# State attention in front of two expert layers on one core: score products on 64x32 array tiles, the state softmax by a GpSimd subtraction and an exponential out of PSUM

## Chip, cores and metric

The kernel runs on one core of one Trainium2 chip. The metric is the device time of one execution in microseconds: the median of 3 runs of the kernel before is 488.5 us (487.32 to 489.64).

## What is computed

Three layers in float32. The first is an attention between tokens and 32 state vectors per head, in both directions; its output, 512 token rows and 32 state rows for each of 8 batches (4608 rows of 512), goes through a soft mixture of 8 experts and then through a gated linear unit.

```python
# x: (8, 8, 512, 64) batches, heads, tokens, width; state: (8, 8, 32, 64)
scores = scale * x @ state.T
a = softmax(scores, axis=-1)           # over the 32 states
xread = a @ state
a2 = softmax(scale * state @ x.T, -1)  # over the 512 tokens
sread = a2 @ x
x = concat([xread, sread], axis=2)     # then rows x (heads * width) = 4608 x 512
logits = x @ phi                       # 32 slots, 4 for each expert
slot_input = softmax(logits, 0).T @ x
slot_out[e] = relu(slot_input[e] @ w1[e]) @ w2[e]
x = softmax(logits, 1) @ slot_out
out = (silu(x @ w_gate) * (x @ w_val)) @ w_out
```

Both softmaxes subtract their maximum and divide by the sum plus 1e-9.

## The kernel before

The order of the work on every engine is the order of the program text: the whole kernel is written under a manual schedule, so that each engine (TensorE, ScalarE, VectorE, GpSimd and SyncE, which issues the loads) carries out its instructions in the order in which the lines call them, and waits by semaphores for what it needs.

**Attention.** The loop of line 979 takes batches b = 0 to 6; a step of it works on batch b and finishes pieces of b-1 and b-2. `scores` (line 232) multiplies stB, the state vectors of a pair of heads laid on the diagonal of a 128x64 block with zeros beside them, with the transposed tokens xT: four products of 512 columns, two on each half of the array's columns. ScalarE copies the scores with the scale into the tile sts (line 240). `load_T` (line 216) makes xT for batches 3 to 7 on chip, by 16 transposes of xn and two copies of 1024 columns, half 0 on VectorE, half 1 on ScalarE (line 230); for batches 0 to 2 it is loaded. From sts two softmaxes start:

- over the tokens (a2): `scores_max` (line 243) takes the negated maximum along the rows on VectorE, `state_exp` (line 248) gives the exponential with that bias and with the sum as accumulator, in two halves on ScalarE, `state_tr` (line 304) transposes the result on TensorE and copies it out, `sread_mm` multiplies it with xn and `sread_out` (line 330) with the reciprocal of the sums, which `sread_recip` (line 311) has made, into srC;
- over the states (a): `attn_sub` (line 263) transposes the scores, takes the maximum over each 32 and subtracts it (two VectorE passes of 1024 columns), `attn_exp` (line 273) gives the exponential on ScalarE, the sum and its reciprocal on VectorE and the normalisation on GpSimd (line 286), `attn_tr` (line 338) transposes a and copies it for the logits.

`logits_mm`, `logits_max`, `logits_exp`, `logits_tr`, `slots_mm` and `slots_out` make the slot softmax of the token rows of a batch, one or two steps later; `sr_T`, `sr_mm`, `sr_exp` and `sr_tr` do it for the state rows, four batches at a time. In batch 0 the product SP of stB and phi is made as well (line 1012). `build_stB` (line 394) fills stB for four batches, by two copies of 64 partitions each. The last batch (from line 1029) is written out by itself: there the softmax over the states goes in halves of 512 columns (`half_sub`, `half_exp`, `half_at`), and the normalisation of half 0 is GpSimd's, of half 1 VectorE's (line 1063).

**PSUM.** `pbig` hands out three buffers of two banks in turn, `psmall` two of one bank.

**Loads.** `push` makes the list of all loads in order: tokens, w1 and w2 of the two expert groups, the weights of the gated unit. `pump` issues what has room: 17 ring places of 8 KB a partition (`rg`), which come free with `done()`, and the tiles named in `spots`, which hold parts of w1 of (group, index) (0, 2) to (0, 7), (1, 0) and (1, 1) in working tiles as they come free; a tag in `late` is not used before `free(tag)` is called. The loads are issued by SyncE in that order.

**Experts.** From line 1198: `expert_1` multiplies the slot inputs with w1, `expert_2` with w2; the first preparations of the gated unit run beside them. **Main loop.** From line 1348: 17 blocks of 256 rows, 6 pairs of column blocks of the gated unit; the change does not touch it, except for the tag of a converted weight tile (line 646).

Of the kernel before, what the change touches and what calls it, by code (L numbers as in the profile page):

```python
# [50 lines left out]
XT_PE = (3, 4, 5, 6, 7)  # L51
ROWS = S + NS
# [13 lines left out]
def attn_moe_glu_kernel(  # L66
# [36 lines left out]
    stB = wk.tile([128, B, 4, 64], F32, tag="A", name="stB")  # L103
# [34 lines left out]
    late = {"x", "A", "a2", "sts", "e2", "a0", "at"}  # L138
# [34 lines left out]
    def push_pair(q):  # L173
# [40 lines left out]
    xT = {}  # L214

    def load_T(b, half):
        if b >= B or b not in XT_PE:
            return
        x_ = got["xn", b]
        if half == 0:  # L220
            xT[b] = rg.tile([128, 4, S], F32, tag="u", name="xT")
            room[0] -= 1
            if b == XT_PE[-1]:
                room[1] = 0
        p = pbig([128, 2, S])
        for kk in range(2):
            kc = 2 * half + kk
            for j in range(4):
                pe.transpose(p[:, kk, j * 128:(j + 1) * 128], x_[:, j, kc * 128:(kc + 1) * 128], ident)
        (act.copy if half else dve.tensor_copy)(out=xT[b][:, 2 * half:2 * half + 2, :], in_=p)  # L230

    def scores(b):
        x_ = xT.pop(b) if b in XT_PE else got.pop(("xt", b))
        p = pbig([128, 2, S])
        for pr in range(4):
            r = 64 * (pr % 2)
            pe.matmul(out=p[r:r + 64, pr // 2, :], lhsT=stB[:, b, pr, :], rhs=x_[:, pr, :], start=True, stop=True)  # L237
        done()
        t = wk.tile([128, 2, S], F32, tag="sts", bufs=1, name="sts")
# [23 lines left out]
    def attn_sub(b):  # L263
        t = sts[b]
        v = tr8([t[:, 0, :], t[:, 1, :]]).rearrange("p j (h s) -> p (j h) s", s=NS)
        m1 = sm.tile([128, 32], F32, tag="m1", name="m1")
        dve.tensor_reduce(out=m1, in_=v, axis=AX.X, op=ALU.max)  # L267
        a = wk.tile([128, 4, 256], F32, tag=f"a{b % 3}", name="a")
        av = a.rearrange("p j (h s) -> p (j h) s", s=NS)
        dve.tensor_tensor(out=av, in0=v, in1=bc(m1, NS), op=ALU.subtract)  # L270
        A[b] = a

    def attn_exp(b, part=True):
        a = A[b]
        av = a.rearrange("p j (h s) -> p (j h) s", s=NS)
        if part is not None:
            act.activation(out=a, in_=a, func=AF.Exp)  # L277
        if part is False:
            return
        z = sm.tile([128, 32], F32, tag="z", bufs=1, name="z")  # L280
        dve.tensor_reduce(out=z, in_=av, axis=AX.X, op=ALU.add)  # L281
# [3 lines left out]
        if part:  # L285
            pool.tensor_tensor(out=av, in0=av, in1=bc(r, NS), op=ALU.mult)  # L286
        else:
            RZ["a"] = r

    def attn_norm(b):  # L290
        av = A[b].rearrange("p j (h s) -> p (j h) s", s=NS)
        dve.tensor_tensor(out=av, in0=av, in1=bc(RZ.pop("a"), NS), op=ALU.mult)
# [11 lines left out]
    def state_tr(b, eng=act):  # L304
        e = E2T.pop(b)
        p = tr8([e[:, 0, :], e[:, 1, :]])
        t = e.rearrange("p q s -> p (q s)").rearrange("p (j n) -> p j n", j=4)
        (act.copy if eng is act else dve.tensor_copy)(out=t, in_=p)
        E2N[b] = t

    def sread_recip(b):
        z = RZ.pop(b)
        dve.tensor_scalar(out=z, in0=z, scalar1=EPS, scalar2=None, op0=ALU.add)
        r2 = sm.tile([128, 2], F32, tag="r2", name="r2")
        dve.reciprocal(out=r2, in_=z)
        RZ[b] = r2

    def sread_mm(b):
        x_, e = got.pop(("xn", b)), E2N.pop(b)
        p = psmall([128, 2, D])  # L320
        for q in range(2):
            for j in range(4):
                for c in range(4):
                    h = 4 * q + c
                    pe.matmul(out=p[32 * c:32 * c + 32, q, :], lhsT=e[:, j, h * 32:h * 32 + 32], rhs=x_[:, j, h * 64:h * 64 + 64],
# [4 lines left out]
    def sread_out(b):  # L330
        p, r2 = P4.pop(b), RZ.pop(b)
        o = 32 * (b % 4)
        for c in range(4):
            dst = srC[o:o + 32, b // 4, :, :].rearrange("p (q c) d -> p q c d", c=4)[:, :, c, :]
            cc = slice(32 * c, 32 * c + 32)
            dve.tensor_tensor(out=dst, in0=p[cc], in1=bc(r2, D)[cc], op=ALU.mult)  # L336
# [57 lines left out]
    def build_stB(g):  # L394
# [3 lines left out]
        v = p.rearrange("p r (b s) -> p b r s", s=NS)  # L398
        for hh in range(2):
            r = slice(64 * hh, 64 * hh + 64)  # L400
            dve.tensor_copy(out=stB[r, 4 * g:4 * g + 4, :, NS * hh:NS * hh + NS], in_=v[r])
# [240 lines left out]
    def split_wo(q, t, sc):  # L642
        if q == 2:
            w = bqm[:, 0:1024].bitcast(F16).rearrange("p (a n) -> p a n", a=2)
        else:
            w = wk.tile([128, 2, 1024], F16, tag=("at", "a2", "", "sts", "C", "stn")[q], bufs=1, name="wo16")
# [305 lines left out]
    with tc.manual_schedule():  # L952
# [10 lines left out]
        dve.memset(stB, 0.0)  # L963
# [15 lines left out]
        for b in range(B - 1):  # L979
# [4 lines left out]
            if ok(b - 1):  # L984
                sread_recip(b - 1)
# [6 lines left out]
            at(b, 1)  # L992
            state_exp(b)
            if ok(b - 1):
# [3 lines left out]
            at(b, 2)  # L998
            attn_sub(b)
            at(b, 3)  # L1000
            if ok(b - 1):
                attn_tr(b - 1)
            at(b, 4)
            state_tr(b)
            at(b, 5)
            attn_exp(b)
            if b == 0:
                p = psmall([128, B, 2, NSL])
                for bb in range(B):
                    for pr in range(4):  # L1010
                        r = 64 * (pr % 2)
# [399 lines left out]
```

## Time and profile before

| | |
|---|---|
| median of 3 runs | 488.5 us |
| the profiled execution | 489.95 us, of which 488.2 us are its span |
| TensorE busy | 461.4 us (95%) |
| VectorE busy | 322.8 us (66%) |
| ScalarE busy | 260.2 us (53%) |
| GpSimd busy | 156.8 us (32%) |
| chain that ended last | TensorE 71%, VectorE 19%, ScalarE 5% of the span |

Busy time is the time in which an engine works on an instruction; matmuls are pipelined, so TensorE's is not the time at its peak. The chain that ended last is followed back from the last instruction of the program to what released each step; an engine's share of it says how much of the span hung on that engine.

### The profile page before, as it was taken

To read this page: it belongs to the slowest core of one execution; us is meant where nothing else is said; L and a number is where in the kernel's file an instruction comes from. 1 tells how busy PE (TensorE), PEld (TensorE's weight loads), DVE (VectorE), ACT (ScalarE), POOL (GpSimd) and SP (SyncE) were. 2 spreads that over 40 slices of the span, in tenths; PEclk is the share of its full clock that TensorE was granted. 3 is DMA by queue.
4 is the path that set the end of the run, shared out by engine and by line. 5 is a ranking of instruction groups with operands and counts; after the bars stand their busy time and mean duration, and the time that the engine had idled before them with its cause. 6 is when DMAs were issued, how large, how long until landed. Compare 5 with 4: busy or idle time off the path is not lost.

```text
span 488.2 us, 9003 instructions
## 1 busy us (share of the span) xinstructions
PE 461.4 (95%) x3543; PEld 253.2 (52%) x3543; DVE 322.8 (66%) x614; ACT 260.2 (53%) x452; POOL 156.8 (32%) x134
## 2 busy tenths in 40 slices
PE   7889999899898999998999899899999999999996
PEld 6666667645355454454455354455555555555553
DVE  3888888657618866768989878876433344344454
ACT  1677676634405988777456365545444444444441
POOL 0111221128013434343343243342433333333331
PEclk9999999999899999999999999999999999999999
DMA  8999985969999820202000000000011112112124
GB/s 300 425 416 411 419 338 207 348 234 367 421 401 418 367 87 2 64 23 79 9 1 1 0 1 0 2 1 1 0 44 43 45 43 68 63 45 76 54 86 173
DMA packets 16363, 74.23 MB, mean 152 GB/s; under 512 B 1601, under 2 KB 3009, under 8 KB 9665
## 3 DMA queue, kind: packets, MB, share of 16 engines
q1 hardware_dynamic: 16320, 73.65, 38.6%
q8 instruction: 28, 0.46, 0.4%
q14 instruction: 15, 0.11, 0.1%
HBM read 64.73 MB, written 8.91 MB: 151 GB/s over the span
## 4 chain that ended last, share of the span: by engine, by line
PE 71%; DVE 19%; ACT 5%; issue 2%; DMA 1%; POOL 0%; SPq 0%; DVEq 0%; ACTq 0%; POOLq 0%
PE p L1296 48%; PE p L1262 8%; PE p L483 3%; PE p L514 3%; DVE nm L245 2%; DMA u<-in_xt_dram 1%; DVE srC L336 1%; DVE sh L1267 1%; DVE gvf L569 1%; DVE a L270 1%; DVE z L281 1%; PE s L734 1%; DVE xT L230 1%; DVE m L267 1%; PE p L237 1%
## 5 line engine op out<-in xcount | busy, mean ns | idle before, releaser
L1296 PE MATMUL p<-wo,hl 128*128 128x512 f16 x1020 | 235.1, 379 | 4.4 <-DVE osb L1307 3.3
L1276 POOL TENSOR_TENSOR hl<-sh,hl 128x512 f16<-128x512 f32 x102 | 125.4, 1229 | 202.4 <-ACT hl L1275 112.8
L1296 PEld LDWEIGHTS <-hl 128*128 128x128 f16 x1224 | 119.1, 98 | 129.9 <-issue 4.6
L1267 DVE SCALAR_TENSOR_TENSOR sh<-p,segk,sh 128x512 f32<-128x512 f32 x102 | 76.4, 749 | 93.8 <-ACT sh L1263 85.3
L1275 ACT CAST hl<-sh 128x512 f16<-128x512 f32 x102 | 62.9, 617 | 115.3 <-PE p L1296 80.9
L1263 ACT ACTIVATE sh<-p,sg 128x512 f32<-128x512 f32 x85 | 58.3, 686 | 5.7 <-PE p L1262 1.0
L1307 DVE SCALAR_TENSOR_TENSOR osb<-p,segm,osb 128x512 f32<-128x512 f32 x62 | 45.3, 747 | 10.9 <-PE p L1296 10.9
L1296 PE MATMUL p<-bqm,hl 128*128 128x512 f16 x204 | 46.8, 379 | 0.0
L1262 PE MATMUL p<-cstack,gvs 128*128 128x256 f16 x272 | 41.2, 273 | 2.4 <-DVE gvs L892 1.3
L1262 PEld LDWEIGHTS <-gvs 128*128 128x128 f16 x272 | 25.9, 98 | 20.5 <-issue 3.2
L286 POOL TENSOR_TENSOR a<-a,r 128x1024 f32<-128x1024 f32 x7 | 13.4, 1914 | 68.1 <-DVE md L363 48.9
L1262 PE MATMUL p<-cstack,gv 128*128 128x256 f16 x136 | 20.6, 273 | 0.9 <-DVE segm L807 0.9
L1305 ACT ACTIVATE osb<-p,segk 128x512 f32<-128x512 f32 x26 | 17.2, 693 | 3.3 <-PE p L1296 3.0
L569 DVE SCALAR_TENSOR_TENSOR gvf<-u,gvf 128x512 uint32<-128x512 uint32 (+1 forms) x22 | 18.6, 860 | 0.1
L1262 PEld LDWEIGHTS <-gv 128*128 128x128 f16 x136 | 13.0, 98 | 10.1 <-issue 1.7
L573 DVE SCALAR_TENSOR_TENSOR gvf<-u,gvf 128x512 uint32<-128x512 uint32 (+1 forms) x22 | 18.1, 843 | 0.1
L514 PE MATMUL p<-u,exq 128*32 128x256 f32 x256 | 15.4, 382 | 0.7 <-ACT exq L504 0.7
L253 ACT ACTIVATE e<-sts,nm 128x512 f32<-128x512 f32 x16 | 11.4, 715 | 8.2 <-DVE nm L245 8.2
L563 ACT ACTIVATE gvf<-u 128x512 f32<-128x512 f32 (+1 forms) x22 | 15.3, 716 | 0.0
L240 ACT ACTIVATE sts<-p 128x1024 f32<-128x1024 f32 x7 | 7.2, 1025 | 12.8 <-PE p L237 12.8
L281 DVE TENSOR_REDUCE z<-a 128x32 f32<-128x1024 f32 x7 | 8.5, 1220 | 8.1 <-ACT a L277 8.1
L566 DVE TENSOR_SCALAR gvf<-gvf 128x512 uint32<-128x512 uint32 (+1 forms) x22 | 12.1, 565 | 1.5 <-ACT gvf L563 1.3
(261 smaller groups left out, 538.0 us busy)
## 6 DMA issues: line engine op xcount, KB each, us to landing
u<-in_w_dram SPq DMA_DIRECT2D x23, 1024.0 KB, 13.8
u<-in_wgv_dram SPq DMA_DIRECT2D x12, 1024.0 KB, 17.0
u<-in_xn_dram SPq DMA_DIRECT2D x8, 1024.0 KB, 16.8
out_dram<-osb SPq DMA_DIRECT2D x15, 512.0 KB, 2.8
early<-in_w_dram SPq DMA_DIRECT2D x14, 512.0 KB, 7.7
u<-in_wo_dram SPq DMA_DIRECT2D x5, 1024.0 KB, 14.1
u<-in_xt_dram SPq DMA_DIRECT2D x3, 1024.0 KB, 8.5
u<-in_wo_dram SPq DMA_DIRECT2D x2, 512.0 KB, 13.2
```

The costliest lines, as they stand in the source:

```text
L514: pe.matmul(out=SO[g][i][32 * j:32 * j + 32, :], lhsT=hT[g, k // 4][:, k % 4, 32 * j:32 * j + 32], rhs=u[:, j, :], start=(k == 0), stop=(k ...
L563: act.activation(out=out_t[:, c], in_=hf[:, c], func=AF.Copy, scale=2.0 ** -112)
L569: dve.scalar_tensor_tensor(out=tu[:, c], in0=lo[:, c], scalar=29, in1=tu[:, c], op0=ALU.logical_shift_right, op1=ALU.bitwise_or)
L573: dve.scalar_tensor_tensor(out=tu[:, c], in0=hi[:, c], scalar=0x80000000, in1=tu[:, c], op0=ALU.bitwise_and, op1=ALU.bitwise_or)
L1262: pe.matmul(out=p[v][:, 256 * i:256 * i + 256], lhsT=GV[2 * q + i][v], rhs=rhs, start=True, stop=True)
L1263: act.activation(out=sh[:, 0, :], in_=p[0], func=AF.Silu, scale=sgs[q])
L1267: dve.scalar_tensor_tensor(out=sh[:, 1, :], in0=p[1], scalar=(kap0[0] if k == 0 else seg_scale(*seg)[0][q]), in1=sh[:, 0, :], op0=ALU.mult ...
L1275: act.copy(out=t[:, 0, :], in_=sh[:, 1, :])
L1276: pool.tensor_tensor(out=t[:, 1, :], in0=sh[:, 1, :], in1=t[:, 0, :], op=ALU.subtract)
L1296: pe.matmul(out=accs[i], lhsT=t[:, u // 2, c], rhs=WO[2 * q + j][:, u % 2, :], start=first and u == 0 and j == 0, stop=last and (j, u) == ...
L1305: act.activation(out=o, in_=a, func=AF.Copy, scale=rsc)
L1307: dve.scalar_tensor_tensor(out=o, in0=a, scalar=rsc, in1=o, op0=ALU.mult, op1=ALU.add)
```

## The change

`scores` multiplies each head by itself: eight products instead of four, each with 64 rows and 32 columns of the array, and stB holds no zeros any more (so that it is half as large, needs no memset, and its tile has room for sts). The two heads of a pair are the two row halves and write to two banks. The state softmax changes: GpSimd adds the negated maximum to sts in place, TensorE transposes the result, ScalarE takes the exponential out of PSUM in one pass, and the sums come out of `sread_mm`: xn, as it is laid out in memory, has a column of ones beside each pair of heads (rows of 520 numbers for 512), and each product takes 65 columns. The scaling by the reciprocal sums stands at the head of `sread_out`. The max, subtraction, exponential and sums of the softmax over the states go in halves for every batch, and the sums and the normalisation stand in `attn_norm`, after `state_tr`. Both copies of `load_T` are ScalarE's. `slots_mm` of b-2 comes before `state_tr`. The w1 block (0, 6) goes to the ring, the second half of (1, 0) to the tile e2 in place of sts, and the tile A is free after the last `state_tr`.

```diff
-    stB = wk.tile([128, B, 4, 64], F32, tag="A", name="stB")
+    atA = wk.tile([128, 2176], F32, tag="A", name="atA")
+    stB = atA[:, 0:1024].rearrange("p (b r s) -> p b r s", b=B, r=4)
+    stsA = atA[:, 1024:2048].rearrange("p (q s) -> p q s", q=2)
...
-        [("sts", 1, "sts"), ("e2", 1, "e2")], [("a0", 1, "a0"), ("at", 1, "at")]))}
-    for i, v in enumerate(([("fr", 1, "x"), ("sts", 1, "x")], [("a2", 1, "x"), ("a0", 1, "x")])[:REUSE]):
+        None, [("a0", 1, "a0"), ("at", 1, "at")])) if v}
+    for i, v in enumerate(([("fr", 1, "x"), ("e2", 1, "e2")], [("a2", 1, "x"), ("a0", 1, "x")])[:REUSE]):
...
-                pe.transpose(p[:, kk, j * 128:(j + 1) * 128], x_[:, j, kc * 128:(kc + 1) * 128], ident)
-        (act.copy if half else dve.tensor_copy)(out=xT[b][:, 2 * half:2 * half + 2, :], in_=p)
+                pe.transpose(p[:, kk, j * 128:(j + 1) * 128], x_[:, j, kc, 1:129], ident)
+        (act.copy, XTE)[half](out=xT[b][:, 2 * half:2 * half + 2, :], in_=p)
+
+    def score_mm(b, x_, p, cols):
+        n = cols.stop - cols.start
+        for pr in range(4):
+            for hh in range(2):
+                r = slice(64 * hh, 64 * hh + 64)
+                pe.matmul(out=p[32 * pr:32 * pr + 32, hh, 0:n], lhsT=stB[r, b, pr, :], rhs=x_[r, pr, cols],
+                          start=True, stop=True)
...
-    def state_exp(b):
-        nm, t = RZ[b], sts[b]
-        e = wk.tile([128, 2, S], F32, tag="e2", name="e2")
-        z2 = sm.tile([128, 2], F32, tag="z2", name="z2")
+    def state_shift(b):
+        nm, t = RZ.pop(b), sts[b]
         for q in range(2):
-            act.activation(out=e[:, q, :], in_=t[:, q, :], func=AF.Exp, bias=nm[:, q:q + 1], accum_out=z2[:, q:q + 1])
-        E2T[b], RZ[b] = e, z2
+            pool.tensor_scalar(out=t[:, q, :], in0=t[:, q, :], scalar1=nm[:, q:q + 1], scalar2=None, op0=ALU.add)
...
+        for i in range(2):
+            vi, ai = (u[:, 2 * i:2 * i + 2, :].rearrange("p j (h s) -> p (j h) s", s=NS) for u in (v, a))
+            m1 = sm.tile([128, 16], F32, tag="m1", name="m1")
+            dve.tensor_reduce(out=m1, in_=vi, axis=AX.X, op=ALU.max)
+            dve.tensor_tensor(out=ai, in0=vi, in1=bc(m1, NS), op=ALU.subtract)
         A[b] = a
 
-    def attn_exp(b, part=True):
+    def attn_exp(b):
+        a = A[b]
+        for i in range(2):
+            act.activation(out=a[:, 2 * i:2 * i + 2, :], in_=a[:, 2 * i:2 * i + 2, :], func=AF.Exp)
+
+    def attn_norm(b):
...
+        for i in range(2):
+            dve.tensor_reduce(out=z[:, 16 * i:16 * i + 16], in_=av[:, 16 * i:16 * i + 16, :], axis=AX.X, op=ALU.add)
         dve.tensor_scalar(out=z, in0=z, scalar1=EPS, scalar2=None, op0=ALU.add)
         r = sm.tile([128, 32], F32, tag="r", bufs=1, name="r")
         dve.reciprocal(out=r, in_=z)
...
+        pool.tensor_tensor(out=av, in0=av, in1=bc(r, NS), op=ALU.mult)
...
+    def state_tr(b):
+        t = sts[b]
+        p = tr8([t[:, 0, :], t[:, 1, :]])
+        e = wk.tile([128, 4, 256], F32, tag="e2", name="e2")
+        act.activation(out=e, in_=p, func=AF.Exp)
+        E2N[b] = e
...
-                    pe.matmul(out=p[32 * c:32 * c + 32, q, :], lhsT=e[:, j, h * 32:h * 32 + 32], rhs=x_[:, j, h * 64:h * 64 + 64],
+                    k = 128 * q + 32 * c
+                    pe.matmul(out=p[32 * c:32 * c + 32, 65 * q:65 * q + 65], lhsT=e[:, j, k:k + 32],
+                              rhs=x_[:, j, c, 65 * q:65 * q + 65],
                               start=(j == 0), stop=(j == 3))
...
-        p, r2 = P4.pop(b), RZ.pop(b)
+        p = P4.pop(b)
+        z = sm.tile([128, 2], F32, tag="z2", name="z2")
+        dve.tensor_scalar(out=z, in0=p[:, 0:130:129], scalar1=EPS, scalar2=None, op0=ALU.add)
+        r2 = sm.tile([128, 2], F32, tag="r2", name="r2")
+        dve.reciprocal(out=r2, in_=z)
...
-        dve.memset(stB, 0.0)
...
             if ok(b - 1):
                 sread_mm(b - 1)
-            at(b, 1)
-            state_exp(b)
-            if ok(b - 1):
                 sread_out(b - 1)
             if ok(b - 2):
                 logits_tr(b - 2)
-            at(b, 2)
             attn_sub(b)
-            at(b, 3)
+            state_shift(b)
             if ok(b - 1):
                 attn_tr(b - 1)
-            at(b, 4)
+            attn_exp(b)
+            if ok(b - 2):
+                slots_mm(b - 2)
             state_tr(b)
-            at(b, 5)
-            attn_exp(b)
+            attn_norm(b)
...
-        free("A")
-        sread_recip(b - 1)
...
         scores_max(b)
+        state_shift(b)
         logits_tr(b - 2)
         sread_mm(b - 1)
-        state_exp(b)
-        free("sts")
         attn_tr(b - 1)
...
         state_tr(b)
+        free("A")
...
-        sread_recip(b)
...
-    xn = x.reshape(B, H, 4, 128, D).transpose(0, 3, 2, 1, 4).reshape(B, 128, 4, H * D)
+    xn = _np.ones((B, 128, 4, H // 2, 2 * D + 2), _np.float32)
+    xn[..., 1:-1] = x.reshape(B, H, 4, 128, D).transpose(0, 3, 2, 1, 4).reshape(B, 128, 4, H // 2, 2 * D)
```

## Rows read from the trace of the kernel before

**Rows 1.** The chain of waits, 0 to 240 us: start, us, what

```profile
8.76 1.95 PE p L237 x8
...
15.64 1.99 PE s L1012 x64
...
19.42 1.03 ACT sts L240
...
30.62 1.13 DVE nm L245
...
46.12 1.06 ACT a L277
...
56.56 1.06 ACT a L277
...
82.57 0.60 DVE m L1041
...
103.06 7.00 PE p L483 x64
...
143.32 0.57 PE p L514 x8
```

**Rows 2.** Busy time by stage: one step of the attention loop, and the experts

```profile
core 0: us, PE busy (x) PEld busy (x) DVE busy (x) ACT busy (x) POOL busy (x), PEclk, DMA share, GB/s
...
41.00:51.40 10.40, 9.35 (x138) 6.74 (x138) 8.91 (x16) 7.62 (x15) 1.91 (x1) 1.00 1.02 409
...
103.00:146.00 43.00, 40.96 (x470) 19.18 (x469) 23.99 (x48) 14.21 (x23) 14.80 (x17) 0.96 0.96 373
```

**Rows 3.** Timeline of one step of the attention loop, 40 to 52 us

```profile
41.31 1.04 PE L260 MATMUL p<-cs,sts 128*128 128x128 f32 x8
...
42.18 1.04 PE L343 MATMUL p<-cs,a 128*128 128x128 f32 x8
...
45.12 0.62 PE L353 MATMUL s<-at,SP 128*32 128x128 f32 x16
...
46.17 1.94 PE L237 MATMUL p<-xT,stB 128*64 128x512 f32 x8 [0.42 <-DVE a L270]
...
49.17 1.23 DVE L230 COPY xT<-p 128x1024 f32<-128x1024 f32 x1
49.27 1.91 POOL L286 TENSOR_TENSOR a<-a,r 128x1024 f32<-128x1024 f32 x1 [8.53 <-DVE md L363]
...
49.93 1.10 PE L325 MATMUL s<-u,e 128*32 128x64 f32 x64
...
50.31 0.90 DVE L313 TENSOR_SCALAR z<-z 128x2 f32<-128x2 f32 x1
50.95 0.40 ACT L368 ACTIVATE le<-le,md 128x128 f32<-128x128 f32 x1
...
51.32 1.20 DVE L245 TENSOR_REDUCE nm<-sts 128x2 f32<-128x1024 f32 x1
51.49 0.14 PEld L374 LDWEIGHTS s<-cs,le 128*128 128x128 f32 x1 [0.39 <-ACT le L368]
```

**Rows 4.** Groups of instructions, 0 to 240 us: busy us, mean ns, idle before

```profile
L336 DVE TENSOR_TENSOR srC<-s,r 32x128 f32<-32x128 f32 x32 | 9.2, 286 | 0.6
...
L240 ACT ACTIVATE sts<-p 128x1024 f32<-128x1024 f32 x7 | 7.2, 1025 | 12.8 <-PE p L237 12.8
...
L457 POOL CAST cc<-cc 128x512 f16<-128x512 f32 x4 | 2.7, 694 | 0.1
...
L672 POOL TENSOR_SCALAR sgn<-u 128x512 f32<-128x512 f32 x1 | 2.0, 1962 | 19.5 <-PE p L514 19.5
...
L1042 DVE TENSOR_TENSOR a<-p,m 128x512 f32<-128x512 f32 x2 | 1.4, 692 | 0.1
...
L1041 DVE TENSOR_REDUCE m<-p 128x16 f32<-128x512 f32 x2 | 1.4, 675 | 0.0
...
L1045 ACT ACTIVATE a<-a 128x512 f32<-128x512 f32 x2 | 1.3, 630 | 3.0 <-DVE a L1042 3.0
```

**Rows 5.** Loads issued from 122.5 to 125 us: size, us to landing

```profile
u<-in_w_dram SPq DMA_DIRECT2D x1, 512.0 KB, 17.9
```

More of the change, by code (lines that the diff above doesn't have):

```diff
@@ L136, in attn_moe_glu_kernel @@
     room = [RING, 1 if XT_PE else 0]
[L138 removed]
+    late = {"x", "A", "a2", "e2", "a0", "at"}
     def pump(n=99):
@@ L214, in attn_moe_glu_kernel @@
     xT = {}
+    XTE = (act.copy, dve.tensor_copy)[XT_DVE]
     def load_T(b, half):
@@ L234, in scores @@
         p = pbig([128, 2, S])
-        for pr in range(4):
-            r = 64 * (pr % 2)
-            pe.matmul(out=p[r:r + 64, pr // 2, :], lhsT=stB[:, b, pr, :], rhs=x_[:, pr, :], start=True, stop=True)
+        score_mm(b, x_, p, slice(0, S))
         done()
-        t = wk.tile([128, 2, S], F32, tag="sts", bufs=1, name="sts")
+        t = stsA
         act.activation(out=t, in_=p, func=AF.Copy, scale=SCALE)
@@ L302, in fill @@
             pe.matmul(out=hz, lhsT=ident, rhs=ident, start=True, stop=True)
[L304 to L316, printed above, removed]
+    def state_tr(b):
[4 more added lines that the diff above has]
+        E2N[b] = e
     def sread_mm(b):
         x_, e = got.pop(("xn", b)), E2N.pop(b)
-        p = psmall([128, 2, D])
+        p = psmall([128, 130])
         for q in range(2):
@@ L397, in build_stB @@
             pe.transpose(p[:, pr, :], stN[:, g, 2 * pr:2 * pr + 2, :].rearrange("p h d -> p (h d)"), ident)
[L398 to L401, printed above, removed]
+        dve.tensor_copy(out=stB[:, 4 * g:4 * g + 4, :, :], in_=p.rearrange("p r (b s) -> p b r s", s=NS))
     SRT, esl = {}, {}
@@ L997, in attn_moe_glu_kernel @@
                 logits_tr(b - 2)
-            at(b, 2)
             attn_sub(b)
-            at(b, 3)
+            state_shift(b)
             if ok(b - 1):
                 attn_tr(b - 1)
-            at(b, 4)
+            attn_exp(b)
+            if ok(b - 2):
+                slots_mm(b - 2)
             state_tr(b)
-            at(b, 5)
-            attn_exp(b)
+            attn_norm(b)
             if b == 0:
-                p = psmall([128, B, 2, NSL])
+                p = pbig([128, 2, 512])
                 for bb in range(B):
                     for pr in range(4):
-                        r = 64 * (pr % 2)
-                        pe.matmul(out=p[r:r + 64, bb, pr // 2, :], lhsT=stB[:, bb, pr, :], rhs=phs[:, pr, :],
-                                  start=True, stop=True)
-                act.copy(out=SP, in_=p)
-            if ok(b - 2):
-                slots_mm(b - 2)
+                        for hh in range(2):
+                            r = slice(64 * hh, 64 * hh + 64)
+                            pe.matmul(out=p[32 * pr:32 * pr + 32, hh, 32 * bb:32 * bb + 32], lhsT=stB[r, bb, pr, :],
+                                      rhs=phs[r, pr, :], start=True, stop=True)
+                act.copy(out=SP.rearrange("p b q s -> p q b s"), in_=p[:, :, 0:256].rearrange("p q (b s) -> p q b s", s=NSL))
             if ok(b - 1):
@@ L1078, in attn_moe_glu_kernel @@
         for i in range(2):
-            p = pbig([128, 2, 256])
-            for pr in range(4):
-                r = 64 * (pr % 2)
-                pe.matmul(out=p[r:r + 64, pr // 2, :], lhsT=stB[:, b, pr, :], rhs=x_[:, pr, 256 * i:256 * i + 256],
-                          start=True, stop=True)
-            act.activation(out=t[:, :, 256 * i:256 * i + 256], in_=p, func=AF.Copy, scale=SCALE)
+            p = pbig([128, 2, 512])
+            score_mm(b, x_, p, slice(256 * i, 256 * i + 256))
+            act.activation(out=t[:, :, 256 * i:256 * i + 256], in_=p[:, :, 0:256], func=AF.Copy, scale=SCALE)
         done()
-        free("A")
-        sread_recip(b - 1)
         half_tr(0)
```

33 lines of the change are left out of this document (7 added, 26 removed).

## The prediction

> **What bounds it now.** I read the chain of waits first. The attention loop is one long chain of VectorE work: the exponential of one batch ends a stretch of VectorE, and the next batch's exponential comes 10.44 us later (46.12 to 56.56) [rows 1]; from the maximum of batch 2 (30.62) to the first step of the last batch (82.57) it is five times 10.39 us [rows 1]. The table by stage says what shares that period: of 10.4 us VectorE is busy for 8.91, TensorE for 9.35, ScalarE for 7.62, GpSimd for 1.91 [rows 2]. VectorE's idle time is one wait for the exponential, and part of its busy time is none: the two-element add of line 313 takes 0.90 us and ends at 51.21, just as GpSimd's normalisation (49.27, 1.91 us) ends at 51.18 [rows 3]. So a period is VectorE's own work, a stall behind GpSimd, and one ScalarE pass. From 103.06 TensorE takes over with the experts, where it is busy for 40.96 of 43 us and DMA for 0.96 of them [rows 1, 2]. Nothing of the diff touches that stage but the places of some loads; time can only be won before 103.
>
> **The parts.** Times are one batch's.
>
> *VectorE.* The copy of half 0 of xT (1.23 us [rows 3]) leaves it and goes to ScalarE, which copies half 1 already. The two halves of max, subtraction and sum cost 2 x (0.675 + 0.692 + 0.675) = 4.1 us [rows 4] where three whole passes of that width stood. The reciprocal and the add for the state sums stay, but the add reads PSUM and no longer falls under GpSimd's normalisation, so I take 0.3 us for both. With the maximum's 1.20 [rows 3], four srC products of 0.286 [rows 4], and 1.0 us of small pieces, VectorE has about 7.8 us, 1.1 less than now; it stops being the bound. The add of the a sums (line 282) is of the kind that was held: a subtraction still running on GpSimd would hold it. By the placing below the subtraction ends 6.8 us after the scores copy starts and that add comes at 8.7, so I take nothing; at p = 1.96 they meet.
>
> *ScalarE.* Gone: two half exponentials with accumulators and the copy after the transposes. New: one exponential of 1024 columns out of PSUM and one more xT copy, each by the copy of that size 1.025 us, and two half exponentials of 0.630 in place of a whole one [rows 4]. About the same sum, but another order, and that order is what counts: scores copy, two xT copies, exponential of logits, copy of the transposed a, exponentials, small copies.
>
> *TensorE.* Four score products on 128x64 tiles take 1.94 us [rows 3]. Eight on 64x32 tiles have half the work for the array if all eight tiles run at once (about 1.0 us, an estimate: half of 1.94), and the same 1.94 if the two row halves go one behind the other. No row of the trace has two row halves at work at once. That column tiles run at once is seen: line 325's 64 products of 64 columns take 1.10 us, 17 ns each, where eight 128-column transposes on the whole array take 1.04, 130 ns each [rows 3]. I take 1.0; the range keeps 1.94. By the Trainium skill, "TensorE: Matmul & The Clock Gate", the section on packing small matmuls, row and column tiles compose; by it the score is 1.0 us too, and no row here shows it. The SP product (64 matmuls for 32, was 1.99 us [rows 1]) lies between 1.0 and 2.0 for the same reason.
>
> *GpSimd.* New: two subtractions of 128x512, p each. It is the dearest unknown. The nearest rows: a cast of 128x512 takes 0.694, the only TENSOR_SCALAR, with two operations, takes 1.962 [rows 4]. Half of the latter is 0.98; one operation with one input is nearer to that and to the cast. I take p = 1.0, and keep 0.69 and 1.96. The Trainium skill, "GPSIMD Engine Reference", section on engine selection, warns against elementwise work there but calls one-input work roughly line-rate; by that p would be about 0.7 (the VectorE row of that width), an estimate, and the sum below would not change, since another chain holds at 9.6.
>
> *The period.* Two chains go round a batch.
> ScalarE: scores copy 1.02, two xT copies 2.03, exponential of logits until its transpose starts 0.54 (50.95 to 51.49), then on TensorE that transpose 0.2 and the transposes of the scores 0.9 and of a 1.04, then the copy of a 1.02, half exponentials 1.26, the state exponential 1.0, two small copies 0.5 [rows 3, 4]: 9.5, with a hand-off or two 9.6. VectorE's part of it (srC, then the halves, then the second half exponential) comes out within 0.1 of it.
> GpSimd: transposes of the scores 1.04, two subtractions 2p, state transposes 1.04, logits 0.62, next score 1.0, its copy 1.02, xT copies 2.03, 0.54 and 0.2 [rows 3, 4]: 7.6 + 2p with hand-offs, 9.6 at p = 1. xT's transposes lie behind the copies.
> So 9.6 for 10.39. What is late next is TensorE's wait for GpSimd's subtraction, with the state transposes, logits and next score queued behind it. The normalisation stands behind the subtraction on GpSimd too; it is due only a batch later, so it is covered, as long as 2p + 1.9 fits in a period.
>
> *The start.* The first score waits for a load at 8.76 as now [rows 1]; the memset and half of a copy (0.69) that go are covered by that load. Then: score to 9.8, copy 10.8, maximum 12.1, stB copy 12.8, halves to 15.5, last half exponential 16.2, state exponential 17.2, SP copy 17.9, and the scores copy of batch 1 starts there, not at 19.42 [rows 1]. Batch 1 has no xT copies and no old logits: copy 1.05, maximum 1.2, srC and its scale 1.55, halves 2.75, exponentials 0.65 and 1.0, small copy 0.25, 8.4 in all; the maximum of batch 2 starts at 27.4, not 30.62: 3.2 us won.
>
> *The end of attention.* 27.4 + 5 x 9.6 = 75.4, and 0.9 for the copies of sr_T and sr_mm that now lie on ScalarE's chain, 0.2 for halves: 76.5 for 82.57, so 6.1 won. In the last batch the subtraction (2.0) starts behind the maximum and ends just before GpSimd gets its half of the normalisation: covered at p = 1, any more is added. The state sums' add and reciprocal, done early until now, come behind the last product: 0.3 lost. Sum: 5.8.
>
> *Loads.* SP's order moves: the load of expert block (0, 4) waits for the state transposes of the last batch in place of its scores (about 8 us later, still some 15 us ahead of its use); (0, 6) takes a ring place, so one 1 MB block more is asked for only when the experts free places, and half of (1, 0) comes earlier: 0.5 MB more in the full stretch, about 1.2 us of DMA. The last w2 half is issued after 122.5 and lands 17.9 us later [rows 5], at 140.4 to 142; its product is at 143.32 [rows 1]. The cover is 1.3 us or more, so this costs nothing; without it up to 1.2. xn rows grow by 1.6%: nothing, their users come later.
>
> The profiled execution took 489.95 us, 1.45 above the median shown; 484.15 against it is **482.7** against 488.5. (0.5%, 2.4 us, is what a measurement of this kernel can tell from no change.)
>
> **Rivals.**
> *Slower: GpSimd's subtraction takes the place of VectorE.* The place is the wait of the state transposes. At p = 1.96 the period is 11.5: 27.9 + 57.5 + 1.1 = 86.5, 4.0 later, and 1.9 for the last normalisation and 0.3: 494.7. It is slower than now from p = 1.48 on. For it: the only row of that operation [rows 4]. Against: that row has two operations and a comparison. 0.20.
> *The row halves don't run together.* Score 1.94: the GpSimd chain is 10.5, the start loses 2.8 of its 3.2: 30.2 + 52.5 + 1.1 = 83.8, with 0.3 and the last batch's score some 2 us slower than now, 490.5. For it: no row with two row halves. 0.13.
> *The gain ends at DMA.* If the weights hold the experts, which DMA's 0.96 speaks for and a single cover of 1.3 us speaks against, what is left is 487 or so. 0.07.
>
> **Numbers.** The forecast has 0.60, from 9.4 to 9.9 a period: 481.5 to 484.5 and, if the clock or the order of waits does better (periods of 9.0), down to 478.5. The range takes in the row rival and p up to 1.7 (P 11.0, 491 to 492): 478.5 to 492. Faster by over 0.5%: 0.61 (forecast and a bit of DMA). Within: 0.18 (half of the row rival, DMA, p from 1.3 to 1.6). Slower: 0.21 (p over 1.6, the other half of the row rival).
>
> **What would show it.** Right: scores copies 9.5 to 9.7 us apart in the middle, score products within about 1.0 us, subtractions of 0.7 to 1.1 us, no DVE add of over 0.3 us, experts from about 97. Wrong: a GpSimd row over 1.4 us with the state transposes waiting for it; score products over 1.7 us; experts early but the main loop no earlier; TensorE's granted clock, at its upper level of 2.4 GHz all through the loop now (1.00 [rows 2]), falling in it.

## The result, and the profile after

The changed kernel takes 492.87 us (median; 491.02 to 494.1) where the kernel before took 487.12 us on the same chip (486.45 to 489.64): a ratio of 1.0099, 95% interval 1.0076 to 1.0123. It is slower by about 1%, and the forecast said 1.2% faster. The execution shown here is the fastest of them, 491.02 us with a span of 489.2.

The table by stage comes first: one step of the attention loop, and the first 40 us of the experts. They answer to [rows 2].

```profile
core 0: us, PE busy (x) PEld busy (x) DVE busy (x) ACT busy (x) POOL busy (x), PEclk, DMA share, GB/s
41.00:51.40 10.40, 8.73 (x148) 6.24 (x147) 7.66 (x17) 7.12 (x14) 5.01 (x4) 1.00 1.02 410
105.91:146.00 40.09, 38.10 (x460) 18.20 (x462) 23.35 (x46) 13.98 (x22) 13.76 (x17) 1.00 0.95 373
```

VectorE fell from 8.91 us of 10.4 to 7.66, TensorE from 9.35 to 8.73, ScalarE from 7.62 to 7.12. GpSimd rose from 1.91 to 5.01. No engine is full, yet the step is as long as before: the score copies start at 39.99, 50.41 and 60.83 us, 10.42 apart, where it was 10.39. Something waits round a ring. The chain of waits (start, us, what) shows it, with the start and the end of the attention stage around it; it answers to [rows 1].

```profile
7.08 1.09 PE p L241 x16
...
15.04 1.22 PE p L1005 x79
...
17.20 0.23 PE s L321 x2
17.43 2.54 issue
19.97 1.11 PE s L321 x62
...
27.50 1.89 PE p L241 x16
...
39.99 0.89 ACT atA L250
...
40.91 1.93 ACT xT L234 x2
42.84 0.40 ACT le L369 x2
...
43.28 0.33 PE s L375
43.61 0.89 PE p L267 x8
...
44.54 1.48 issue
46.02 1.57 POOL atA L261
...
47.64 0.98 PE p L267 x7
48.62 0.57 PE s L354 x16
49.20 1.02 PE p L241 x16
...
84.02 0.70 DVE m L1030
...
88.06 3.12 POOL atA L261 x2
...
105.91 2.33 PE p L481 x17
```

Read the ring from 39.99: the score copy, two xT copies and the logit exponentials on ScalarE; the logit transposes and the score transposes on TensorE; then the two subtractions on GpSimd, the first under the name "issue" (44.54, 1.48), the second at 46.02; the state transposes, the logits, the next batch's score, and its copy at 50.41. The subtractions take 3.11 us of it, the rest 7.31. Attention ends 1.45 us later (84.02 for 82.57), and the experts begin at 105.91 for 103.06, 2.85 later.

The timeline of the same step says who waited for whom, and the groups of 0 to 240 us (busy us, mean ns of one, idle before) what each operation costs; they answer to [rows 3, 4].

```profile
44.48 3.11 POOL L261 TENSOR_SCALAR atA<-atA,nm 128x512 f32<-128x512 f32 x2 [3.41 <-PE p L267]
...
47.64 0.98 PE L267 MATMUL p<-cs,atA 128*128 128x128 f32 x7 [1.21 <-POOL atA L261]
...
49.13 1.09 PE L241 MATMUL p<-xT,atA 64*32 64x512 f32 x16
```

```profile
L261 POOL TENSOR_SCALAR atA<-atA,nm 128x512 f32<-128x512 f32 x16 | 24.9, 1566 | 37.7 <-PE p L267 17.7 <-DVE srC L337 15.3 <-DVE nm L255 4.7
...
L330 DVE TENSOR_SCALAR z<-s 128x2 f32<-128x2 f32 x8 | 1.3, 159 | 4.6 <-PE s L321 4.6
```

One subtraction takes 1.566 us. The score of a batch takes 1.09 us for 1.94, and the small add of the state sums 0.159 us where line 313 took 0.90 [rows 3].

### The profile page after: what moved, and what is told of

Its sections match the earlier page's. It is cut to its first block, busy times and chain, and to the rows that moved or that the text cites. A ratio compares the mean times of both kernels' runs of the same rounds, so it can differ in the third digit from the quotient of the medians.

```text
span 489.2 us, 9283 instructions
## 1 busy us (share of the span) xinstructions
PE 455.3 (93%) x3679; PEld 249.1 (51%) x3679; DVE 313.4 (64%) x627; ACT 254.6 (52%) x432; POOL 182.2 (37%) x150
## 3 DMA queue, kind: packets, MB, share of 16 engines
HBM read 64.87 MB, written 8.91 MB: 151 GB/s over the span
## 4 chain that ended last, share of the span: by engine, by line
PE 78%; DVE 10%; issue 4%; POOL 3%; ACT 2%; DMA 1%; SPq 0%; ACTq 0%; DVEq 0%; POOLq 0%
PE p L1279 49%; PE p L1245 8%; POOL atA L261 3%; PE p L512 3%; PE p L481 3%; PE p L267 2%; PE p L241 2%; PE p L233 2%; PE s L321 1%; DVE sh L1250 1%; DVE gvf L567 1%; PE s L732 1%; DMA u<-in_xt_dram 1%; DVE srC L337 1%; PE s L354 1%
## 5 line engine op out<-in xcount | busy, mean ns | idle before, releaser
L261 POOL TENSOR_SCALAR atA<-atA,nm 128x512 f32<-128x512 f32 x16 | 24.9, 1566 | 37.7 <-PE p L267 17.7
L267 PE MATMUL p<-cs,atA 128*128 128x128 f32 x120 | 18.0, 283 | 12.9 <-POOL atA L261 11.3
L267 PEld LDWEIGHTS p<-cs,atA 128*128 128x128 f32 x120 | 13.5, 141 | 17.4 <-POOL atA L261 17.3
L255 DVE TENSOR_REDUCE nm<-atA 128x2 f32<-128x1024 f32 x8 | 9.7, 1218 | 14.0 <-ACT atA L250 14.0
```

The source lines that it names most:

```text
L261: pool.tensor_scalar(out=t[:, q, :], in0=t[:, q, :], scalar1=nm[:, q:q + 1], scalar2=None, op0=ALU.add)
L267: pe.transpose(p[:, j, q * 128:(q + 1) * 128], src[q][:, j * 128:(j + 1) * 128], ident)
```

## The experiments

The theory after this result (A): the subtractions sit in TensorE's in-order path, and their price sets the period. Its rival (B): ScalarE, which now has both xT copies, holds it. Four kernels tell them apart.

**The subtraction left out.**

```diff
-        for q in range(2):
-            pool.tensor_scalar(out=t[:, q, :], in0=t[:, q, :], scalar1=nm[:, q:q + 1], scalar2=None, op0=ALU.add)
```

> The changed kernel without the state softmax's subtraction (the exponential is taken of the unshifted scores; the maximum is still computed, and nothing uses it). Theory A (the two GpSimd subtractions, 3.11 us a batch, stand on TensorE's in-order path between the transposes of the scores and the state transposes): the period of the loop falls from 10.42 us to about 9.5, where ScalarE's chain holds it, the last batch loses a wait of 1.4 us, and the kernel is 5 to 8 us faster than the changed kernel (487.1 to 485). Theory B (ScalarE with both xT copies holds the period, and GpSimd only ends at about the same time): the period stays at 10.3 to 10.4 and at most 2 us are won.

Measured: 480.55 us, ratio to before 0.9823 (0.977 to 0.9876), copies 9.17 apart, experts from 94.74. The period is theory A's; the time fell by more than its 5 to 8 us (12.3 between the medians). Its chain of waits in the loop:

```profile
45.37 1.95 ACT xT L234 x2
47.32 0.40 ACT le L367 x2
...
48.09 0.89 PE p L265 x8
...
49.00 0.70 DVE m L275
...
51.78 0.63 ACT a L282
```

With p = 0 the other chain of the prediction is left: ScalarE's copies, the score transposes, VectorE's halves, ScalarE's exponentials.

**The subtraction on VectorE**, ahead of the halves.

```diff
-            pool.tensor_scalar(out=t[:, q, :], in0=t[:, q, :], ...)
+            dve.tensor_scalar(out=t[:, q, :], in0=t[:, q, :], ...)
...
         attn_sub(b): tr8(...)
+        state_shift(b)
```

> The changed kernel with the subtraction on VectorE, ahead of the two halves of the maximum over the states. Theory A: two instructions of about 0.47 us (the shift of line 566 of the kernel before, 128x512 in SBUF) in place of 3.11 us; VectorE's 7.66 us a batch become 8.6, the period 9.5 to 9.9, the kernel 4 to 7 us faster than the changed one. Theory B: period 10.3 to 10.4, at most 2 us.

Measured: 486.45 us, ratio 0.9958 (0.9928 to 0.9987), copies 9.85 apart. The group of the subtraction:

```profile
L261 DVE TENSOR_SCALAR atA<-atA,nm 128x512 f32<-128x512 f32 x16 | 7.0, 482 | 0.8 <-PE p L267 0.5
```

The same operation on the same operands takes 0.482 us on VectorE for 1.566 on GpSimd. Both together stand in that other chain, between the score transposes and the halves, with 0.88 us (41.34); the period is 0.68 longer than without a subtraction, and the kernel still beats before, by 0.4%.

**Half of xT back on VectorE.**

```diff
-XT_DVE = 0
+XT_DVE = 1
```

> The changed kernel with one half of xT copied by VectorE again. Theory A: ScalarE comes 1.0 us earlier to the exponential of the logits, but TensorE is not there before the product for sread is done, so the period falls by 0.3 us at most and the kernel by 0 to 2 us. Theory B: the period falls by about 1.0 us, to 9.4, and the kernel by some 5 us.

Measured: 494.27 us, ratio 1.0102 (1.005 to 1.0153), copies 10.20 apart for 10.42. Taking a copy from ScalarE wins 0.22 us a step, within theory A's 0.3 and far from theory B's 1.0, and no time. Its chain of waits shows why: the maximum now stands behind the copy on VectorE, and the subtraction waits for the maximum.

```profile
43.86 1.22 DVE xT L234
45.09 1.14 DVE nm L255
...
46.38 3.11 POOL atA L261 x2
```

**Both halves in one instruction of another kind**: one add of two tensors, with the maximum broadcast.

```diff
-        for q in range(2):
-            pool.tensor_scalar(out=t[:, q, :], in0=t[:, q, :], scalar1=nm[:, q:q + 1], scalar2=None, op0=ALU.add)
+        pool.tensor_tensor(out=t, in0=t, in1=bc(nm, S), op=ALU.add)
```

> The changed kernel with the subtraction as one GpSimd TENSOR_TENSOR of 128x1024 with the maximum broadcast, in place of two TENSOR_SCALAR of 128x512. Theory A: it takes 1.92 us like the normalisation of that size, against 3.11, so the period falls by 0.9 to 1.2 us (to 9.3 to 9.5) and the kernel by 5 to 6 us. Theory B: the period stays.

Measured: 485.81 us, ratio 0.9936 (0.9909 to 0.9963), copies 9.40 apart, experts from 98.01. The group:

```profile
L260 POOL TENSOR_TENSOR atA<-atA,nm 128x1024 f32<-128x1024 f32 x8 | 15.1, 1892 | 31.5 <-PE p L266 27.8 <-DVE nm L255 3.7
```

1.89 us for 3.11: 1.22 us less, and the period falls by 1.02. With this one price lower by two fifths, and nothing else touched, the change that lost 1% wins 0.6%.

The second question is the start. TensorE stands still for 2.54 us in the middle of the first state read (17.43 in the chain above), and nothing that the profile shows holds it. Theory C: instructions come late at that place of the program; rival D: a wait of the state read itself. The next four kernels build on the cheaper subtraction, which has the same stop (2.58 us).

**Twelve short products more ahead of the first score.** (Each product leaves two records here; the texts on record that speak of 128 small products of SP mean its 64 products, 128 records.)

```diff
         heat(HB, 2)
+        for _ in range(12):
+            pe.matmul(out=hz0[:, 0:32], lhsT=ident, rhs=ident[:, 0:32], start=True, stop=True)
```

> The subtraction as one broadcast add, plus twelve matmuls of 32 columns more in the wait before the first score product (work added, nothing left out). Theory C, the 2.5 us stop of TensorE after the 2nd product of the first state read belongs to a place in TensorE's instruction stream (instructions that come late): the stop moves 12 matmuls earlier in the program, out of the state read and to the products ahead of it, and is still 2 to 3 us. Rival D, it is a wait of the state read itself (an operand or an output buffer): the stop stays after the same product of the state read. Either way the span stays within 1 us of the 484.8 of the run without the twelve.

Measured: one time, 488.05 us, span 486.3, 1.5 us above the 484.8 where less than 1 was expected: the added products kept TensorE for 2.87 us (7.49), the granted clock fell to 0.72 from 9 to 15 us, and the first score copy came at 12.35 us for 8.40. The twelve products are 24 records, and the stop went back by 23 (2 of the state read, 16 of the score, 5 of SP), out of the state read and into the SP product. The timeline of TensorE:

```profile
18.63 1.24 PE L1007 MATMUL p<-phs,atA 64*32 64x32 f32 x123
21.52 0.26 PE L1007 MATMUL p<-phs,atA 64*32 64x32 f32 x5 [1.65 <-issue]
```

So D falls and C holds: the stop belongs to a place in TensorE's stream. (Its size, 1.65 us, is below C's 2 to 3.) Batch 1, free of the stop and at the full clock from 18 us on, takes 8.19 us from copy to copy (22.90 to 31.09).

**The SP product in batch 1 instead of batch 0.**

```diff
-            if b == 0:
+            if b == 1:
                 p = pbig([128, 2, 512])
```

> The subtraction as one broadcast add, and the softmax constants of the state passages (the 128 small products of SP) made in batch 1 instead of in batch 0; nothing left out. Theory C (late instructions): no stop in the first state read, which ends some 1.3 us earlier for the products moved and up to 2.5 us earlier for the stop; the score copy of batch 2 comes 1.5 to 3.5 us before its 36.8 us, and the time falls from 485.8 to 483 to 484.5. Rival D (a wait of the state read): the stop stays after its 2nd product, the copy of batch 2 comes at most 1.3 us earlier, the time is 485 to 486.

Measured: 485.26 us, ratio 0.9954 (0.993 to 0.9978). The stop left the state read and stands in batch 2, 40 records behind the SP product's new place:

```profile
26.52 1.09 PE L233 MATMUL p<-cs,u 128*128 128x128 f32 x8
29.57 1.03 PE L233 MATMUL p<-cs,u 128*128 128x128 f32 x8 [1.96 <-issue]
```

The place is C's, the gain isn't: the copy of batch 2 starts at 26.75 for 27.39, then the stop delays batch 3's to 38.18 for 36.76 (the 36.8 that the expectation gives to batch 2 is batch 3's), and the time is rival D's, 485 to 486.

**The logit exponentials ahead of xT's two copies on ScalarE**, with the cheaper subtraction. (The texts on record say "ahead of the score copy"; the edit puts them between it and xT's copies.)

```diff
             scores(b)
-            at(b, 0)
             if ok(b - 2):
                 logits_exp(b - 2)
+            at(b, 0)
```

> The subtraction as one broadcast add, and the exponentials of batch b-2's logits placed on ScalarE ahead of batch b's score copy and its two transposed copies instead of behind them; nothing left out. Theory A2 (with the cheaper subtraction the period of 9.40 is a loop through TensorE, ScalarE's transposed copies and VectorE's halves, in which the slot transposes wait for logit exponentials that stand behind two copies of 0.95 us): period 8.7 to 9.1, the experts begin some 2 us earlier, time 483 to 484.5. Rival (the period is set by TensorE's own 8.7 us of work and the order in it): period 9.3 to 9.5, time 485.5 to 486.5.

Measured: 481.86 us, ratio 0.9863 (0.9835 to 0.9891), copies 8.91 and 8.90 apart, experts from 95.67. This beats both kernels and is the best seen with nothing left out. Its chain of waits runs over TensorE and GpSimd alone:

```profile
46.98 1.04 PE s L320 x64
48.02 0.37 PE s L374 x2
48.39 0.89 PE p L266 x8
...
49.35 1.90 POOL atA L260
```

**Both moves together** (the two diffs above).

> Both moves: the small products of SP in batch 1 and the logit exponentials ahead of the score copy, with the subtraction as one broadcast add; nothing left out. By theories A2 and C together the gains add: period 8.7 to 9.1, time 480 to 483, below the kernel before by 1.2 to 1.8%. If C falls, the time is that of the run with the exponentials moved alone, within 1 us.

Measured: 483.36 us, ratio 0.9899 (0.9872 to 0.9927). The period is 9.04 and 8.91, but a stop of 1.79 us stands in batch 2 and the third copy comes at 37.30, later than without the move (36.72). The gains don't add: 480 to 483 was expected, and the time is no better than with the exponentials moved alone.

**The SP product in four parts of 32**, on the best kernel, for a new theory (E): the run of 128 short records outpaces the supply of instructions.

```diff
-            if b == 0:
+            if b < 4:
                 p = pbig([128, 2, 512])
-                for bb in range(B):
+                for bb in (2 * b, 2 * b + 1):
...
-                act.copy(out=SP..., in_=p[:, :, 0:256]...)
+                act.copy(out=SP[:, 2 * b:2 * b + 2]..., in_=p[:, :, 64 * b:64 * b + 64]...)
```

> The fastest so far (subtraction as one broadcast add, logit exponentials ahead of the score copy), with the 128 small products of SP split: 32 in each of the batches 0 to 3 in place of 128 in a row in batch 0, with four small copies in place of one; nothing left out. Theory E, the stop of TensorE comes from the run of 128 short products, which uses up instructions faster than they are brought in while the loads fill the DMA engines: no stop over 0.6 us in the first 40 us, the score copy of batch 2 at 24.5 to 26 us in place of 27.45, time 479 to 481. Rival F, the stop falls wherever a new stretch of the program begins, however dense the products: a stop of 1.5 to 3 us remains, at another product, and the time is 481 to 482.5.

Measured: 483.11 us, ratio 0.9908 (0.9878 to 0.9939). E was right about the stop (0.20 us is left) and the copy of batch 2 (25.74 for 27.45), and wrong about the time. The lead of 1.7 us is gone by the copy of batch 4 (45.71 for 45.63). The timeline of TensorE shows what took it: in the steps of batches 2 and 3 a part of SP stands on TensorE's path, and it waits first for the second subtraction of VectorE's halves.

```profile
33.90 0.36 PE L1004 MATMUL p<-phs,atA 64*32 64x32 f32 x32 [0.39 <-DVE a L277]
...
43.56 0.36 PE L1004 MATMUL p<-phs,atA 64*32 64x32 f32 x32 [0.40 <-DVE a L277]
```

Wait and products make some 0.75 us, and these steps take 10.28 and 9.69 us for the best kernel's 9.27 and 8.91. (By the code the part writes to the next `pbig` buffer, which is the one that the halves read.) The clock alone doesn't explain it. It falls here, and the next score takes 1.96 us for 1.09:

```profile
21.00:24.00 3.00, 1.92 (x56) 1.22 (x64) 2.67 (x6) 2.17 (x5) 0.00 (x0) 0.76 1.01 424
24.00:27.00 3.00, 3.00 (x28) 1.50 (x13) 0.49 (x2) 1.28 (x4) 1.91 (x1) 0.67 1.02 424
```

But the best kernel has such a stretch too, 0.60 and 0.83 from 18 to 24 us.

**The same split on the changed kernel as it is** (the same diff on its lines).

> The changed kernel as it is, with its two subtractions of 1.57 us, and SP made in four parts of 32 products; nothing left out. Theory E: no stop in the first state read, the score copy of batch 2 at 26.5 to 27.5 us in place of 29.58, the period unchanged at 10.4, time 490 to 491 for 492.9. Rival F: the stop stays at another place, the copy of batch 2 at 28.5 or later, time 492 to 493.

Measured: 491.82 us, ratio to before 1.0082 (1.0053 to 1.011). A stop of 0.40 us is left, batch 2 at 28.29 for 29.58, between the two expectations. The clock fell to 0.57 from 15 to 18 us and to 0.56 from 24 to 27, and the steps with a part of SP took 10.78 and 10.71 us, not 10.4. What the stop costs the changed kernel in time isn't settled by this: the two ratios, 1.0082 and 1.0099, lie within each other's intervals.

**The logit exponentials first, on the changed kernel as it is.**

> The changed kernel as it is, with its two subtractions of 1.57 us, and the logit exponentials ahead of the score copy; nothing left out. Theory A (while GpSimd needs 3.1 us a batch, GpSimd and TensorE make the period and ScalarE's order has nothing to give): period 10.3 to 10.5, time 492 to 494. Theory B2 (ScalarE's order was worth 0.5 us a batch whatever GpSimd does): period 9.8 to 10.0, time 489 to 490.5.

Measured: 489.81 us, ratio 1.0032 (1.0008 to 1.0055), copies 9.91 apart. Theory A as it was put there falls: GpSimd's price and ScalarE's order lie in one ring, and either shortens it. Its chain of waits, where logit transposes and score transposes now follow the state read at once:

```profile
40.77 1.04 PE s L321 x64
41.82 0.37 PE s L375 x2
42.19 0.78 PE p L267 x7
...
44.59 1.57 POOL atA L261
```

Less the subtractions, the ring is 10.42 - 3.11 = 7.31 in the changed kernel and 9.40 - 1.90 = 7.50 with the cheaper one; with the order changed it is 9.91 - 3.11 = 6.80 and 8.91 - 1.90 = 7.01. The order is worth 0.5 us a batch with either subtraction, and the subtraction 1.0 with either order.

**The state read behind the score transposes**, on the best kernel, to take its products out of the ring.

```diff
-            if ok(b - 1):
-                sread_mm(b - 1)
-                sread_out(b - 1)
-            if ok(b - 2):
-                logits_tr(b - 2)
             attn_sub(b)
             state_shift(b)
+            if ok(b - 1):
+                sread_mm(b - 1)
+                sread_out(b - 1)
+            if ok(b - 2):
+                logits_tr(b - 2)
```

> The fastest so far (subtraction as one broadcast add, logit exponentials ahead of the score copy), with batch b-1's state read and the transposes of b-2's logits placed on TensorE and VectorE behind batch b's score transposes and halves instead of ahead of them; nothing left out. Theory A2 (the period is a ring: score copy, the products that stand ahead of the score transposes on TensorE, those transposes, the subtraction in place, the transposes of its result, the next score): 1.4 us of products leave the ring, which would be 7.5, and TensorE's own 8.4 to 8.7 us of work takes over: period 8.6 to 8.8, time 479.5 to 481.5 if nothing else waits. Rival G, the ring closes through the logits and the state sums on VectorE instead, whose results now come later: period 8.9 to 9.5, time 482 to 485.

Measured: 493.8 us, ratio 1.0114 (1.0085 to 1.0143), copies 12.19 and 10.67 apart: rival G, and worse than it said. The timeline:

```profile
44.98 0.29 DVE L381 COPY edn<-s 128x128 f32<-128x128 f32 x1
...
45.32 0.64 PE L388 MATMUL s<-a,edn 128*32 128x256 f32 x8 [2.36 <-DVE edn L381]
...
48.13 1.96 PE L241 MATMUL p<-xT,atA 64*32 64x512 f32 x16
```

GpSimd is done early (40.76 to 42.65), but the copy edn now stands behind VectorE's halves; the slot products wait 2.36 us for it, and the state transposes stand behind them on TensorE. The score at 48.13 then runs at the lower clock (1.96 us).

## Why the prediction was wrong, step by step

**The failed step is the price of the subtraction**: "I take p = 1.0, and keep 0.69 and 1.96". It is 1.566. The text had the point from which that decides (1.48), the place (the state transposes wait for GpSimd) and the ring, term by term; the chain of the changed kernel is that ring in that order, with 7.31 us besides the subtractions where the text had 7.6. So the first rival happened. Its chance of 0.20 was too low: with bounds of 0.69 and 1.96 and the break-even at 1.48 inside them, and with the only row of that very operation at 1.962, p = 1.0 leaned on a cast, another operation. At p = 1.57 the rival's own prices give 488.5 + (494.7 - 488.5) x (1.57 - 1.48) / (1.96 - 1.48) = 489.7. So of the 10.2 us between the forecast and the result 7.0 come from p; the 3 us up to 492.9 lie mainly at the start, the second term that failed.

By the Trainium skill, "GPSIMD Engine Reference", Engine selection, one-input work on GpSimd is roughly line-rate. The runs disagree: 1.566 us against VectorE's 0.482 for the same instruction, and more per column than the two-input add (1.892 us for twice the columns). (VectorE was busy beside all 16 subtractions, for most of each; whether GpSimd is faster alone, no run shows.)

**The start** was to win 3.2 us. The score copy of batch 1 did come early (17.38; the text had 17.9, by another way: the first score starts with its load at 7.08 for 8.76, which paid for the dearer subtraction; why the load lands earlier isn't shown). Then batch 1 was to take 8.4 us and took 12.20 (17.38 to 29.58); before it took 7.95 (19.42 to 27.37). In those 12.20 lie the stop of 2.54, 1.1 of dearer subtractions, and a score at half the clock (1.89 for 1.09): 4.4 us, of which 3.8 show. The maximum of batch 2 starts at 30.64, as before (30.62). Without a stop or a clock fall the 8.4 holds: 8.19 in the run with twelve products more, at p = 0.95. But the start isn't the same in every execution: two runs on other chips, half of xT back and exponentials first on the changed kernel, have the same program up to the score copy of batch 2, and there that of batch 1 comes at 18.85 and 19.25 for 17.38 and that of batch 2 at 31.95 and 29.15. So a difference of 1 or 2 us at the start between two profiles shows nothing by itself.

**The SP product** was priced by its own time (1.0 to 2.0; it is 1.29). What it did to the products behind it wasn't seen: it is now 128 records in a row where it was 64, and behind them TensorE stands still (the last section tells where).

**The end of attention** was to come 6.1 us earlier and comes 1.45 later. "Covered at p = 1, any more is added" was right: the last two subtractions stand in the chain with 3.12 us (88.06). From the last whole score copy to the experts it is 34.08 us for 33.61.

**From the experts on** nothing was to change. The experts start 2.85 us later, the profiled span is 1.0 longer: the rows of before show a granted clock of 0.96 over that stage [rows 2], this execution 1.00. The medians differ by 5.8 us; the other executions ran at a mean clock of 0.981 to 0.990 for this one's 0.997. Where in them the rest goes was not seen, since only this one has a profile. The two runs just named show likely places: a granted clock of 0.56 and 0.55 from 15 to 18 us, and of 0.50 again within 130 to 161 us, where this execution has 1.00.

**Right**: VectorE at 7.8 us (7.66) no longer the bound; the score at 1.0 us (1.09), by which the rival of the row halves falls, and which agrees with the Trainium skill, "TensorE: Matmul & The Clock Gate", on packing small matmuls; the small add no longer held (0.159); the ScalarE chain as the one that is left without the subtraction, though at 9.17 and not 9.6; the time there, 480.55, is 2 us below the forecast's 482.7. One reading was off and changed nothing: the 64 of line 325 are records of 32 products, 34 ns each, still far below the transposes' 130. The loads cost nothing: no DMA piece stands in the chain between 92 and 160 us, and the best kernel's experts, 7.4 us earlier than before, keep 7.0 of them in the span, so the rival of DMA falls too.

**Open**: what makes the granted clock fall near the start. It came with the stop and without it, mostly after TensorE had stood waiting, but not after every wait; in the run with twelve products more it fell while TensorE was busy with them (2.94 of the 3 us before 9).

## What to carry to other kernels

Where an unknown price lies on an engine's in-order path and its break-even lies between the bounds, that price is the forecast: give the two sides chances by where the break-even lies, and take the row of the same operation ahead of rows of other kinds. Work moved to an idle engine is free only if nobody waits for it in turn; write the ring out, then look for any member of it that can go first (here an exponential worth 0.5 us a batch) or for another instruction for the same work (1.0 us). Moving a member back in the order moves the work behind it as well: the state read put off cost 12 us against the best.

## What the runs showed of the hardware

On GpSimd the add of a column to 128x512 took 1.566 us, and the add of two tensors 128x1024, one of them broadcast, 1.892: less per column by two fifths. Eight products on 64x32 tiles took 1.09 us where four on 128x64 tiles took 1.94.

**Where TensorE stops for nothing.** Counted in product records from the first state transposes of batch 0 (those 8 included), the stops of the runs lie at two places of the stream, however the work is ordered. The last column counts from the end of a transfer of the instruction queue, q8, to the first product behind the stop:

```
run                                  records before the stop      stop, us     after the transfer, us
changed kernel                       8+128+16+2           = 154   2.54         1.21
  half of xT back; exponentials first  the same           = 154   1.91, 1.80   1.35, 1.47
cheaper subtraction                  the same             = 154   2.58         1.30
  exponentials first                   the same           = 154   2.76         1.36
subtraction left out; on VectorE     8+128+16+3           = 155   2.92, 1.68   1.37, 1.46
state read put off                   8+128+16+3           = 155   0.92, behind a wait of 1.24   1.37
twelve products (24 records) ahead   8+123                = 131   1.65         1.54
SP in batch 1                        8+16+64+8+8+8+128+16+16+8          = 280   1.96   1.52
SP in batch 1, exponentials first    the same             = 280   1.79         1.39
SP in four parts, best kernel        8+32+16+64+8+8+8+32+16+16+16+56    = 280   0.20   1.37
SP in four parts, changed kernel     the same             = 280   0.40         1.49
```

154 and 280 are 126 apart, and the page of the changed kernel (busy time, then the DMA queues) gives the same number from another side:

```profile
PE 455.3 (93%) x3679; PEld 249.1 (51%) x3679; DVE 313.4 (64%) x627; ACT 254.6 (52%) x432; POOL 182.2 (37%) x150
...
q8 instruction: 29, 0.48, 0.4%
```

3679 product records and 3679 of weight loads in 29 transfers are 254 for each: 127 product records with their loads. (Each transfer is 16384 bytes in the trace, 65 for each of the 254. That the queue is TensorE's is inferred from this count and from where the stops lie.) The stop of the changed kernel lasts from 17.43 to 19.97; the DMA view of 17 to 18 us has one such transfer, from 17.76 to 18.76, and those of 15 to 17 and of 18 to 20 us none:

```profile
q8 instruction: 1, 0.02, 6.2%
```

So TensorE's stream comes in pieces of some 127 records, and the stop stands at the seam of two. That the wait is for the transfer is shown as far as times can: the stops differ from 0.20 to 2.92 us, and all of them end 1.2 to 1.5 us behind the end of a transfer. Where all or most of the 128 short records (1.29 us for all of them) lie in the piece that ends at the seam, the stop is 1.65 to 2.92 us (0.92 where a wait came just before it), and the same program up to there gave 1.80 to 2.54; where SP lies in parts of 32, it is 0.2 to 0.4. At 154 none is seen in the runs with SP put off or in parts, and none in the kernel before with its 64 records. That the next piece is asked for too late for a piece used up so fast fits all of this; the request itself is in no view, so it stays an inference. That the loads slow the transfer is not seen: it takes 1.00 us here, and 0.9 to 1.4 in the main loop, where DMA is mostly idle.

**The clock.** In every profile of a changed kernel the granted clock falls to about half, 1.2 GHz for 2.4, at least once within the first 30 us; in the kernel before it doesn't. The changed kernel's score at 27.50 took 1.89 us in such a stretch, for 1.09. The place isn't fixed by the program: of three runs that are the same up to the score copy of batch 2, the changed kernel has 0.81 and 0.62 from 24 to 30 us, half of xT back 0.56 from 15 to 18, 0.51 from 21 to 24 and 0.65 from 27 to 30, and exponentials first on the changed kernel 0.55 from 15 to 18.
